# A linear-attention and token/channel mixer kernel: both first batches' units ahead of the first channel steps, group 0 split around group 1, w_ch1 loaded by step

## The chip, the cores and the metric

One Trainium2 chip; the program runs on one of its cores. The metric is device time in microseconds (us), the median of three runs. The inputs are single precision, the four weight matrices double precision.

## What is computed

```python
q_s = softmax(q, axis=-1)                          # q, k, v: (8, 8, 576, 64)
k_s = softmax(k, axis=2)
kv = np.einsum('bhsd,bhse->bhde', k_s, v)
x = np.einsum('bhsd,bhde->bhse', q_s, kv)          # then (8, 576, 512)
xt = x.transpose(0, 2, 1)
h = np.maximum(xt @ w_tok1, 0.0) @ w_tok2          # 576 -> 256 -> 576
u = x + h.transpose(0, 2, 1)
h2 = np.maximum(u @ w_ch1, 0.0) @ w_ch2            # 512 -> 1536 -> 512
return (u + h2).astype(np.float32)
```

The softmaxes are written out in the reference with a maximum, exponential and a sum plus 1e-9.

## The kernel before

**Units.** Attention and the token mixing are done per unit: a batch b and a pair j of heads, 128 columns of the 512. There are 8 x 4 = 32 units, numbered n = 4 b + j. A unit loads kt, q, k and v (`load_unit`), does the softmaxes (`softmax_k`, `softmax_q`, together `soft`), and then has four stages on TensorE (PE), `pe_stages`: s1 turns q and forms kv, s2 is the product with w_tok1, s3 the hidden layer and the first part of u, s4 the second part of u. Values are split into a high and a low part (`split`: an ACT copy, a VectorE subtraction), and each product is three matmuls. Units 0 to 7 (`on_pe`) transpose k and q on PE and do all subtractions on VectorE (DVE); the later ones turn q on DVE (L262, L270) and give two tensor operations, k_t (L202) and ql (L89), to GpSimd (POOL).

**Groups and steps.** The channel mixing runs over the 8 x 576 = 4608 tokens in nine groups of 512. A batch has 576 tokens, so group g needs u of batch g and, from group 1 on, of the batch before. A group has 12 channel steps f: `ch1` is 12 matmuls of 512 wide into a bank ps_h, then a ReLU on ACT (h2h) and DVE's low part (h2l, L344); `ch2` is 12 matmuls onto four banks ps_o, which hold the group's sums over all twelve steps. ch2 runs one step behind ch1. At the end `residual` adds u's two parts on POOL into a staging tile, and `out_end` adds the bank on DVE and writes out.

**Weights.** Each weight piece (128 x 512 doubles, 512 KB, 29 pieces) goes into a staging tile and is narrowed by five DVE passes and one of ACT (`narrow`, L143 to L150), then split (ACT and DVE). w_ch1 lies in c1h and c1l by rows of 512 columns, w_ch2 by step.

**Order.** Units 0 to 3 come first, with w_tok1, w_tok2 and the first quarter of w_ch1. Then group by group: the units of batch g + 1 are spread over the steps of group g by the table `todo` (one every three steps), and during group 0 each step also loads one piece of w_ch2 and, for eight steps, one of w_ch1. The program is written in that order; a scheduler sets the final order of each engine's queue, and every queue, SP's of loads among them, runs in order. v has a ring of two tiles. Staging and narrowing buffers: two, and two more in pools (`stg_more`, `cv_more`) that are closed when the space is needed. The names and lines that the prediction follows are the DVE passes above, h2l (L344), hl (L296), ul (L329), POOL's ql, k_t and residual (L360), and v_ring.

Of the kernel before, what the change touches and what calls it, by code (L numbers as in the profile page):

```python
# [12 lines left out]
ALU = mybir.AluOpType  # L13
# [7 lines left out]
def attn_mixer_kernel(ctx: ExitStack, tc: tile.TileContext, q, k, kt, v, wt, out, dims):  # L21
# [24 lines left out]
    upool = ctx.enter_context(tc.tile_pool(name="upool", bufs=3))  # L46
# [31 lines left out]
    c1h = const.tile([P, NJ, DCH], F32R, name="c1h")  # L78
    c1l = const.tile([P, NJ, DCH], F32R, name="c1l")
# [145 lines left out]
    def stage_kv(u):  # L225
        kx, vt = u["k"], u["v"]
# [72 lines left out]
    uT = {}  # L299

    def u_tiles(g):
        if g not in uT:
            uT[g] = tuple(upool.tile([P, NJ, CW], F32R, name="u" + part) for part in "hl")
        return uT[g]

    def stage_u(u, half):
# [40 lines left out]
    def ch2(acc, f, hh, hl):  # L347
# [197 lines left out]
```

## Time and profile before

| | |
|---|---|
| median of 3 runs | 860.49 us (858.84 to 860.98) |
| the profiled execution | 860.69 us, span 858.6 us |
| PE matmuls | busy 814.3 us (95%), 4224 instructions |
| DVE | busy 494.7 us (58%), 1093 |
| ACT | busy 335.6 us (39%), 785 |
| POOL | busy 124.4 us (14%), 98 |
| DMA | 63.5 MB, mean 74 GB/s |
| mean granted TensorE clock | 0.982 |

Shares are means over a program with two parts: in the first fifth DVE is full and PE is not, later it is the other way. Matmuls overlap, and a busy PE need not be at its peak; the distance between the starts of matmuls says more than their durations. The same holds for DVE, where an instruction's duration is some 0.07 us longer than the distance to the next start.

### The profile page before, as it was taken

How to read it: one execution, taken by the hardware profiler on the slowest of the kernel's cores; microseconds unless marked ns; L12 is line 12 of the kernel's file. 1: busy time of each engine (PE TensorE's matmuls, PEld its weight loads, DVE VectorE, ACT ScalarE, POOL GpSimd, SP SyncE). 2: the span in 40 equal slices, each digit the busy share in tenths (PEclk: the TensorE clock that was granted, in tenths of full speed). 3: DMA queues.
4: the chain of work that ended last, by engine and by line, in shares of the span. 5: the costliest groups of instructions: out<-in, count | busy, mean ns of one | idle time of the engine just before them, and what ended most of it. 6: DMA issues, size and time to landing. Idle time of an engine off the chain costs nothing.

```text
span 858.6 us, 11201 instructions
## 1 busy us (share of the span) xinstructions
PE 814.3 (95%) x4224; PEld 695.5 (81%) x4224; DVE 494.7 (58%) x1093; ACT 335.6 (39%) x785; POOL 124.4 (14%) x98
## 2 busy tenths in 40 slices
PE   3668999998999999999999999999999999999997
PEld 2567787877888888888888888888888888888886
DVE  7999998966555755485557555765556332112112
ACT  5676664534434444344444443444434331111100
POOL 0000000422011411041113111311132102001100
PEclk9689999999999999999999999999999999999999
DMA  8435444331112311131122112321121001001001
GB/s 285 133 100 179 146 129 162 94 109 60 60 60 71 99 47 55 37 108 61 60 59 98 59 60 60 110 61 60 45 94 45 1 1 50 1 0 50 1 1 49
DMA packets 41685, 63.50 MB, mean 74 GB/s; under 512 B 3488, under 2 KB 22048, under 8 KB 41632
## 3 DMA queue, kind: packets, MB, share of 16 engines
q1 hardware_dynamic: 36448, 53.36, 19.8%
q10 hardware_dynamic: 5184, 9.44, 2.9%
q8 instruction: 33, 0.54, 0.3%
q14 instruction: 20, 0.16, 0.1%
HBM read 53.35 MB, written 9.44 MB: 73 GB/s over the span
## 4 chain that ended last, share of the span: by engine, by line
PE 79%; DVE 13%; DMA 4%; issue 1%; ACT 1%; POOL 1%; SPq 0%; DVEq 0%; POOLq 0%; ACTq 0%
PE ps_h L341 31%; PE ps_o L352 31%; PE ps_h L322 7%; PE ps_h L281 5%; PE ps_h L229 3%; DMA stg<-in_w 2%; DVE cv_s L145 1%; PE ps_h L289 1%; DVE stg L148 1%; DVE cv_s L150 1%; DVE q_t L270 1%; DMA q_t<-in_q 1%; DVE stg L146 1%; DVE cv_s L143 1%; DVE q_t L212 1%
## 5 line engine op out<-in xcount | busy, mean ns | idle before, releaser
L344 DVE SCALAR_TENSOR_TENSOR h2l<-ps_h,h2h 128x512 fp32r<-128x512 f32 x108 | 74.2, 687 | 182.9 <-ACT h2h L343 182.9
L341 PE MATMUL ps_h<-uh,c1h 128*128 128x512 f32 x432 | 172.6, 400 | 0.9 <-ACT k_t L193 0.7
L341 PE MATMUL ps_h<-ul,c1h 128*128 128x512 f32 x432 | 171.7, 397 | 0.4 <-DVE ul L329 0.4
L341 PE MATMUL ps_h<-uh,c1l 128*128 128x512 f32 x432 | 171.4, 397 | 0.0
L352 PE MATMUL ps_o<-h2h,c2l 128*128 128x512 f32 x432 | 169.0, 391 | 0.0
L343 ACT ACTIVATE h2h<-ps_h 128x512 fp32r<-128x512 f32 x108 | 64.4, 597 | 261.1 <-PE ps_h L341 250.5
L352 PE MATMUL ps_o<-h2h,c2h 128*128 128x512 f32 x432 | 165.1, 393 | 1.5 <-DVE stg L367 1.5
L352 PE MATMUL ps_o<-h2l,c2h 128*128 128x512 f32 x432 | 157.3, 396 | 0.0
L270 DVE COPY q_t<-cv_s 32x160 f32<-32x160 f32 (+1 forms) x264 | 73.3, 278 | 69.9 <-POOL ql L89 66.7
L202 POOL TENSOR_TENSOR k_t<-k_t,mb 128x640 f32<-128x640 f32 x24 | 37.7, 1572 | 459.7 <-ACT mb L201 307.6
L341 PEld LDWEIGHTS ps_h<-ul,c1h 128*128 128x128 f32 x432 | 82.0, 190 | 19.8 <-DVE ul L329 0.6
L341 PEld LDWEIGHTS ps_h<-uh,c1h 128*128 128x128 f32 x432 | 82.2, 190 | 17.5 <-ACT k_t L193 0.9
L352 PEld LDWEIGHTS ps_o<-h2h,c2h 128*128 128x128 f32 x432 | 80.7, 188 | 18.6 <-DVE stg L367 2.6
L341 PEld LDWEIGHTS ps_h<-uh,c1l 128*128 128x128 f32 x432 | 82.2, 190 | 16.5
L352 PEld LDWEIGHTS ps_o<-h2h,c2l 128*128 128x128 f32 x432 | 81.1, 188 | 16.1
L352 PEld LDWEIGHTS ps_o<-h2l,c2h 128*128 128x128 f32 x432 | 79.5, 188 | 15.7
L360 POOL TENSOR_TENSOR stg<-uh,ul 128x512 f32<-128x512 f32 x36 | 47.5, 1343 | 128.4 <-DMA out<-stg 76.6
L211 DVE TENSOR_REDUCE st<-q_t 128x10 f32<-128x640 f32 x32 | 26.2, 819 | 43.8 <-DMA q_t<-in_q 43.8
L89 POOL TENSOR_TENSOR ql<-q_t,qh 128x640 fp32r<-128x640 f32 x24 | 37.9, 1581 | 83.7 <-ACT qh L88 64.1
L229 PEld LDWEIGHTS ps_h<-v_ring,k_t 128*128 128x128 f32 x320 | 44.5, 203 | 4.7 <-ACT qtl L253 2.0
L229 PE MATMUL ps_h<-v_ring,k_t 128*128 128x129 f32 x320 | 46.0, 289 | 1.4 <-ACT qtl L253 1.4
L213 ACT ACTIVATE q_t<-q_t 128x640 f32<-128x640 f32 x32 | 23.7, 740 | 49.7 <-DVE q_t L212 49.7
(136 smaller groups left out, 1223.3 us busy)
## 6 DMA issues: line engine op xcount, KB each, us to landing
stg<-in_w SPq DMA_DIRECT2D x28, 512.0 KB, 3.8
kt_t<-in_kt SPq DMA_DIRECT2D x32, 320.0 KB, 3.2
q_t<-in_q SPq DMA_DIRECT2D x32, 320.0 KB, 2.9
out<-stg ACTq DMA_DIRECT2D x36, 256.0 KB, 2.2
v_ring<-in_v SPq DMA_DIRECT2D x32, 256.0 KB, 2.9
k_t<-in_k SPq DMA_DIRECT2D x24, 320.0 KB, 3.4
v_ring<-in_v SPq DMA_DIRECT2D x32, 32.0 KB, 3.1
stg<-in_w SPq DMA_DIRECT2D x1, 256.0 KB, 6.2
```

Of the source, the lines that this page charges most:

```text
L89: lo_eng.tensor_tensor(lo, src, f32(hi), op=ALU.subtract)
L202: nc.gpsimd.tensor_tensor(kx, kx, mb.unsqueeze(1).broadcast_to([P, C1, P]), op=ALU.subtract)
L211: nc.vector.tensor_reduce(st[:, 0, :], qt, axis=AX.X, op=ALU.max)
L229: nc.tensor.matmul(kv[:, 0 : P + 1], kx[:, c, :], vt[:, c, 0 : P + 1], start=(c == 0), stop=(c == C))
L270: eng(qx[ys, 0:n, xs], turned[xs, 0:n, ys])
L281: nc.tensor.matmul(y[:, 0:TOK], a, w, start=(i == 0), stop=(i == len(mm) - 1))
L322: nc.tensor.matmul(t[:, 0:N], a, w, start=(i == 0), stop=(i == len(mm) - 1))
L341: nc.tensor.matmul(t, a[:, n, fs], w, start=(i == 0), stop=(i == 3 * NJ - 1))
L343: nc.scalar.activation(hh, t, AF.Relu)
L344: nc.vector.scalar_tensor_tensor(hl, t, 0.0, f32(hh), op0=ALU.max, op1=ALU.subtract)
L352: nc.tensor.matmul(o, a[:, cs], w, start=(f == 0 and i == 0), stop=(f == NF - 1 and i == 2))
L360: nc.gpsimd.tensor_tensor(res[n // 2][:, n % 2, :], f32(uh), f32(ul), op=ALU.add)
```

## The change

Units 0 to 7, both first batches, come before the first channel step. The steps are then a list: the first four of group 0 (`F_HEAD`), all twelve of group 1, the other eight of group 0, and groups 2 to 8 as before. Group 0's sums of its first four steps are copied by ACT from the banks to a tile `part`; POOL adds u's two parts to it, and the sums of the other eight are added at the end. The units of batch 2 begin ten steps before group 2 and come every two steps; later ones as before. A step's columns of w_ch1 form one piece, and `load_ch(f)` loads that and w_ch2's piece together: two such pairs among the units, one in each of the four first steps, and one in each of the first six of group 1. There is one v tile instead of two, loaded after the kv matmuls of the unit before; the first part has three staging buffers instead of four; the u tiles get fixed slots.

```diff
-    NE = NJ
-    N_PE = 2 * NJ
-    F_MORE = 8
+    NE = 2 * NJ
+    F_HEAD, F_MORE = 4, 8
...
-    NV = 2
-    v_ring = [const.tile([P, C1, P + 1], F32, name=f"v_ring{i}") for i in range(NV)]
+    v_t = const.tile([P, C1, P + 1], F32, name="v_t")
...
+    c2_rows(0, F_HEAD)
+    part = const.tile([P, NJ, CW], F32, name="part")
...
+    def load_v(n):
+        if n < NU:
+            nc.sync.dma_start(v_t[:, 0:C, 0:P], v[n][:, 0:C, :])
+            nc.sync.dma_start(v_t[0:TL, C, 0:P], v[n][0:TL, C, :])
...
+    def load_ch(f):
+        h_, l_ = (w[:, f].rearrange("p n m -> p (n m)") for w in (c1h, c1l))
+        split(h_, l_, load_weights(AT_C1 + f), nc.vector)
         split(*c2[f], load_weights(AT_C2 + f), nc.vector)
...
             nc.tensor.matmul(kv[:, 0 : P + 1], kx[:, c, :], vt[:, c, 0 : P + 1], start=(c == 0), stop=(c == C))
+        load_v(u["n"] + 1)
...
+        uh, ul = (x[:, n, :] for x in uT[g])
+        if g == 0:
+            t = part[:, n, :]
+            nc.gpsimd.tensor_tensor(t, t, f32(uh), op=ALU.add)
+            nc.gpsimd.tensor_tensor(t, t, f32(ul), op=ALU.add)
+            res[n] = t
+            return
...
-    def out_end(g, acc):
+    def out_end(g, acc, whole):
         for n, o in enumerate(acc):
-            t = res[n // 2][:, n % 2, :]
-            nc.vector.tensor_tensor(t, o, t, op=ALU.add)
-            nc.scalar.dma_start(out[g, n], t)
+            if not whole:
+                nc.scalar.copy(part[:, n, :], o)
+                continue
+            nc.vector.tensor_tensor(res[n], o, res[n], op=ALU.add)
+            nc.scalar.dma_start(out[g, n], res[n])
...
+    stg_more = early_pools.enter_context(tc.tile_pool(name="stg_more", bufs=1))
+    conv[:] = [(stg, cv), (stg, cv), (stg_more, cv)]
...
-        if n == NE - 2:
-            load_ch1(0, range(NJ))
+        if n >= NE - 3 and n < NE - 1:
+            load_ch(n - (NE - 3))
...
+    steps = [(0, f) for f in range(F_HEAD)] + [(1, f) for f in range(NF)] + [(0, f) for f in range(F_HEAD, NF)]
+    n0 = len(steps)
+    steps += [(g, f) for g in range(2, NG) for f in range(NF)]
...
+        if b == 2:
+            at = (n0 - 10, n0 - 9, n0 - 9, n0 - 8) if j == 0 else [n0 - 9.5 + 2 * j + x for x in (0, 0.5, 1, 1.5)]
+        else:
+            at = [n0 + (b - 3) * NF + 3 * j + x for x in (0, 1, 1.5, 2)]
...
+    for i, (g, f) in enumerate(steps):
+        if to_load < NF and (i < F_HEAD or g == 1):
...
+            load_ch(to_load)
+            to_load += 1
```

The order of the instructions shows the move. On PE, where the first channel step begins: before, this is behind unit 2 and in the middle of unit 3 (L281 and L322 are a unit's stages, L252 its transposes, L341 is ch1).

```order
L322 MATMUL ps_h<-w2h,hl 128x256
L289 MATMUL ps_h<-kvf,ys 128x128 x2
L322 MATMUL ps_o<-qth,kvh 128x320
L322 MATMUL ps_o<-qtl,kvh 128x320
L322 MATMUL ps_h<-qth,kvh 128x256
L322 MATMUL ps_h<-qtl,kvh 128x256
L341 MATMUL ps_h<-uh,c1h 128x512
L341 MATMUL ps_h<-uh,c1l 128x512
L341 MATMUL ps_h<-ul,c1h 128x512
```

In the change it is in the middle of unit 7, with one operation of unit 8 (L205) already ahead of it; L327 is the unit's stage, L345 is ch1.

```order
L327 MATMUL ps_h<-w2h,hl 128x256
L296 MATMUL ps_h<-kvf,ys 128x128 x2
L327 MATMUL ps_o<-qth,kvh 128x320
L327 MATMUL ps_o<-qtl,kvh 128x320
L327 MATMUL ps_h<-qth,kvh 128x256
L327 MATMUL ps_h<-qtl,kvh 128x256
L205 MATMUL ps_o<-dg,ones 128x128
L345 MATMUL ps_h<-uh_115,c1h 128x512
L345 MATMUL ps_h<-uh_115,c1l 128x512
L345 MATMUL ps_h<-ul_116,c1h 128x512
```

The same ten matmuls of a unit's end stand there, four units later.

On POOL, its first operations on tensors before: k_t and ql of units 8 and 9, and between them the residuals of group 0 (the first two pairs) and of group 1 (the third and fourth).

```order
L202 TENSOR_TENSOR k_t<-k_t,mb 128x640
L360 TENSOR_TENSOR stg<-uh,ul 128x512 x2
L89 TENSOR_TENSOR ql<-q_t,qh 128x640
L360 TENSOR_TENSOR stg<-uh,ul 128x512 x2
L202 TENSOR_TENSOR k_t<-k_t,mb 128x640
L360 TENSOR_TENSOR stg<-uh,ul 128x512 x2
L89 TENSOR_TENSOR ql<-q_t,qh 128x640
L360 TENSOR_TENSOR stg<-uh,ul 128x512 x2
```

In the change: ql and k_t of unit 8, eight additions onto part, four residuals of group 1, k_t and ql of unit 9, and one residual of group 2 at a time.

```order
L97 TENSOR_TENSOR ql<-q_t,qh 128x640
L208 TENSOR_TENSOR k_t<-k_t,mb 128x640
L363 TENSOR_TENSOR part<-part,uh_115 128x512 x3
L364 TENSOR_TENSOR part<-part,ul_116 128x512
L363 TENSOR_TENSOR part<-part,uh_115 128x512
L364 TENSOR_TENSOR part<-part,ul_116 128x512 x3
L370 TENSOR_TENSOR stg<-uh_117,ul_118 128x512 x4
L208 TENSOR_TENSOR k_t<-k_t,mb 128x640
L97 TENSOR_TENSOR ql<-q_t,qh 128x640
L370 TENSOR_TENSOR stg<-uh_119,ul_120 128x512
L208 TENSOR_TENSOR k_t<-k_t,mb 128x640
L97 TENSOR_TENSOR ql<-q_t,qh 128x640
```

Where pairs of residuals stood around unit 9's ql, four additions stand ahead of it, and four more instructions ahead of those.

On DVE, around the change's first h2l (L348; L334 is ul, of unit 7 here, the others are weight passes):

```order
L348 SCALAR_TENSOR_TENSOR h2l<-ps_h,h2h 128x512
L154 SCALAR_TENSOR_TENSOR cv_s<-stg,cv_s 128x512
L152 TENSOR_SCALAR cv_s<-stg 128x512
L334 TENSOR_TENSOR ul_118<-ps_o,uh_117 128x320
L157 SCALAR_TENSOR_TENSOR stg<-stg 128x512
L154 SCALAR_TENSOR_TENSOR cv_s<-stg,cv_s 128x512
L334 TENSOR_TENSOR ul_118<-ps_h,uh_117 128x128
```

This h2l is instruction 232 of DVE's queue counted with repeats; before, the first h2l is instruction 174, and from the first to the thirteenth h2l the change has 119 instructions.

## Rows read from the trace of the kernel before

**Rows 1.** The page: the span in 40 slices of 21.5 us, busy tenths and granted clock

```profile
PE   3668999998999999999999999999999999999997
...
DVE  7999998966555755485557555765556332112112
...
PEclk9689999999999999999999999999999999999999
```

**Rows 2.** Stretches: us, busy us (count) of PE, PEld, DVE, ACT, POOL, clock, DMA, GB/s

```profile
20.00:40.00 20.00, 13.66 (x61) 11.86 (x62) 20.00 (x47) 13.52 (x28) 0.00 (x0) 0.57 0.41 133
740.00:760.00 20.00, 20.00 (x88) 16.22 (x88) 2.20 (x4) 2.39 (x4) 0.00 (x0) 1.00 0.00 1
```

**Rows 3.** Who PE waited for, 0 to 200 us: us in total, times, longest

```profile
PE ps_h L289 <- ACT kvf L236: 7.7, 2, 5.7
...
PE ps_o L352 <- DVE stg L367: 1.5, 3, 0.6
```

**Rows 4.** Timeline of PE, last matmul of units 7 to 10: start us, us, what

```profile
170.97 0.28 PE L322 MATMUL ps_h<-w2h,hl 128*128 128x256 f32 x1
...
199.37 0.30 PE L322 MATMUL ps_h<-w2h,hl 128*128 128x256 f32 x1
...
223.38 0.28 PE L322 MATMUL ps_h<-w2h,hl 128*128 128x256 f32 x1
...
245.85 0.28 PE L322 MATMUL ps_h<-w2h,hl 128*128 128x256 f32 x1
```

**Rows 5.** Timeline of POOL, DVE and PE behind group 0 [idle before it, and until whom]

```profile
188.93 2.54 POOL L360 TENSOR_TENSOR stg<-uh,ul 128x512 f32<-128x512 f32 x2 [6.90 <-DMA out<-stg]
...
193.01 4.80 DVE L270 COPY q_t<-cv_s 32x160 f32<-32x160 f32 x11 [4.72 <-POOL ql L89]
...
198.33 0.41 PE L322 MATMUL ps_h<-w2h,hl 128*128 128x320 f32 x1 [2.17 <-DVE hl L296]
```

**Rows 6.** Timeline of DVE around the first step's h2l

```profile
82.55 0.68 DVE L344 SCALAR_TENSOR_TENSOR h2l<-ps_h,h2h 128x512 fp32r<-128x512 f32 x1
83.16 0.42 DVE L143 TENSOR_SCALAR cv_s<-stg 128x512 uint32<-128x512 uint32 x1
...
84.16 0.80 DVE L182 TENSOR_REDUCE mc<-kt_t 128x1 f32<-128x640 f32 x1
84.88 0.68 DVE L150 TENSOR_TENSOR cv_s<-stg,cv_s 128x512 f32<-128x512 f32 x1
```

**Rows 7.** Stretch up to 170.97 us, ch1 (L341) alone, then ch2 (L352) alone

```profile
0.00:170.97 170.97, 37.72 (x144) 27.39 (x144) 0.92 0.48 154
...
0.00:170.97 170.97, 32.86 (x127) 22.78 (x127) 0.92 0.48 154
```

**Rows 8.** Timeline of POOL and of DVE, 160 to 169 us

```profile
160.50 2.72 POOL L360 TENSOR_TENSOR stg<-uh,ul 128x512 f32<-128x512 f32 x2 [4.40 <-DVE cv_s L150]
163.18 2.01 POOL L89 TENSOR_TENSOR ql<-q_t,qh 128x640 fp32r<-128x640 f32 x1
166.42 3.00 POOL L360 TENSOR_TENSOR stg<-uh,ul 128x512 f32<-128x512 f32 x2 [1.23 <-DVE cv_s L150]
...
160.93 1.14 DVE L146 TENSOR_SCALAR stg<-stg 128x512 uint32<-128x512 uint32 x1
162.11 1.67 DVE L148 SCALAR_TENSOR_TENSOR stg<-stg 128x512 f32<-128x512 uint32 x1
163.70 2.04 DVE L89 TENSOR_TENSOR c2l<-cv_s,c2h 128x512 fp32r<-128x512 f32 x1
...
167.03 1.24 DVE L89 TENSOR_TENSOR c2l<-cv_s,c2h 128x512 fp32r<-128x512 f32 x1
```

**Rows 9.** Tile v_ring, its DMAs; kv matmuls of units 2 and 3 on PE

```profile
DMA to landing us min/median/max: 2.6/3.0/7.3
...
48.31 1.28 PE L229 MATMUL ps_h<-v_ring,k_t 128*128 128x129 f32 x10
...
61.18 2.15 PE L229 MATMUL ps_h<-v_ring,k_t 128*128 128x129 f32 x10
```

More of the change, by code (lines that the diff above doesn't have):

```diff
@@ L297, in stage_h1 @@
         u["hh"], u["hl"] = hh, hl
[L299 to L304, printed above, removed]
+    slots = [tuple(upool.tile([P, NJ, CW], F32R, name=f"u{x}{i}") for x in "hl") for i in range(3)]
+    uT = [slots[i] for i in (0, 1, 2, 1, 0, 2, 1, 0, 2)]
+    assert len(uT) == NG
     def stage_u(u, half):
@@ L345, in ch1, with ch2 @@
         return hh, hl
-    def ch2(acc, f, hh, hl):
+    def ch2(acc, f, first, last, hh, hl):
         for n, o in enumerate(acc):
@@ L414, in attn_mixer_kernel @@
     begin(1)
[L415 removed]
     for n in range(NE):
[L417 removed]
+        st = pe_stages(n)
         st[0]()
         begin(n + 2)
[L420 removed]
+        if n + 1 < NE:
+            soft(n + 1)
         st[1]()
@@ new lines, in attn_mixer_kernel @@
+    for n in range(NE, NU):
+        b, j = divmod(n, NJ)
+        if b == 2:
+            at = (n0 - 10, n0 - 9, n0 - 9, n0 - 8) if j == 0 else [n0 - 9.5 + 2 * j + x for x in (0, 0.5, 1, 1.5)]
+        else:
+            at = [n0 + (b - 3) * NF + 3 * j + x for x in (0, 1, 1.5, 2)]
+        s1, s2, s3, s4 = pe_stages(n)
+        put(at[0], s1)
+        put(at[0], lambda n=n: soft(n + 1))
+        put(at[0] + 0.5, lambda n=n: begin(n + 2))
+        for x, fn in zip(at[1:], (s2, s3, s4)):
+            put(x, fn)
@@ new lines, in attn_mixer_kernel @@
+    pend = None
+    to_load = 2
+    for i, (g, f) in enumerate(steps):
+        if to_load < NF and (i < F_HEAD or g == 1):
+            if to_load == F_MORE:
+                more_pools.close()
+                conv[:] = [(stg, cv)]
+                c2_rows(F_MORE, NF)
+            load_ch(to_load)
+            to_load += 1
+        h = ch1(g, f)
+        for fn in todo.pop(i, []):
+            fn()
+        if pend is not None:
+            ch2(*pend[1:])
+            if pend[0] != g:
+                out_end(*pend[:2], i != F_HEAD)
+        for fn in todo.pop(i + 0.5, []):
+            fn()
+        last = i + 1 == len(steps) or steps[i + 1][0] != g
+        if pend is None or pend[0] != g:
+            acc = [ps_o.tile([P, CW], F32, name="ps_o") for _ in range(NJ)]
+        pend = (g, acc, f, pend is None or pend[0] != g, last, *h)
+        if last and i != F_HEAD - 1:
+            for n in range(NJ):
+                residual(g, n)
@@ L502, in pieces @@
     cut += list(tail)
-    for x in range(0, w_ch1.shape[1], CW):
-        cut += list(w_ch1[:, x : x + CW].reshape(-1, P, CW))
+    n, f = (x // P for x in w_ch1.shape)
+    cut += list(w_ch1.reshape(n, P, f, P).transpose(2, 1, 0, 3).reshape(f, P, CW))
     cut += list(w_ch2.reshape(-1, P, CW))
```

116 lines of the change are left out of this document (31 added, 85 removed).

## The prediction

> **What bounds the kernel now.** I read the page's first two parts, then stretches of 20 us, then who PE waited for, then single lines around the places that these pointed to.
>
> The slices show two stretches: for the first eight DVE is at 9 of 10 or nearly, and PE is short of it in the first four; behind the ninth PE stands at 9 to the end and DVE eases [rows 1]. From 20 to 40 us DVE is busy for all 20 us, PE for 13.66 at a granted clock of 0.57; from 740 to 760 us PE is busy throughout at 1.00, with 88 matmuls, one start every 0.227 us [rows 2]. What fills DVE is narrowing the double-precision weights (six passes a piece and one to split it) and the softmaxes of the first units. So there is a front of some 170 us paced by DVE, and then a long stretch paced by PE. The change has exactly as many matmuls of each shape, so only the front and the hand-over can give time.
>
> PE's waits of the first 200 us are many and small, the largest 7.7 us on kvf [rows 3]. They are links of one chain behind DVE's order; removing one alone gives nothing.
>
> The hand-over shows in the last matmul of each unit: 170.97 us for unit 7, 199.37, 223.38 and 245.85 for units 8 to 10 [rows 4]. The last step is 22.5 us, that of the steady part (three channel steps and a unit); the two before it are 28.4 and 24.0. So 5.9 + 1.5 = **7.4 us are lost around the end of group 0**. How can be read: POOL starts on the residual of group 1 at 188.93, after 6.90 us for an output's DMA to free the staging buffer; the ql of the next unit stands behind it; DVE waits 4.72 us for that ql, then copies the turned q for 4.80 us; hl comes behind the copies, and PE, which had idled 2.17 us for hl, goes on at 198.33 [rows 5].
>
> **The change, step by step.** The profiled execution took 860.69 us with a span of 858.6; the median of the three runs, 860.49, is 0.2 below it, so I sum against 860.7 and take the result for the median's.
>
> *Units 4 to 7 before the first step.* DVE reaches the first step's h2l at 82.55 us [rows 6]. In its order this is the 174th instruction, in the change the 232nd. The 58 more are 21 of 640 wide (6 maxima of kt, 6 reductions and 6 products on q, 3 ql), 5 weight passes (3 long, 2 short), 4 hl, 9 ul, 4 kvl and 15 of a few elements. Start to start, a 640-wide one takes 0.72 us, a 512-wide one 0.61, a short pass some 0.35 (0.42, of which 0.07 overlap) [rows 6]: 15.1 + 1.8 + 0.7, and for the narrow ones, scaled by width, an estimated 1.3 + 2.4 + 0.8 + 2.0. That is 24.1 us; 58 at the full window's mean (47 in 20 us [rows 2]) give 24.7. DVE has no idle time there to absorb it, so the first h2l moves by 24.3 to **106.9 us**. Unit 7's last matmul feeds, by an ACT copy, a ul that stands six rows, some 3 us, behind this h2l: it runs at about 109 us.
>
> *The steps after it.* When unit 7's last matmul runs today, at 170.97 us, PE has issued all 8 units and 144 + 127 = 271 of the steps' matmuls [rows 7]. In the change it has the 8 units and 12 of those at 109 us and needs 259 more: at 0.227 us, 58.8. If nothing stops it, it stands at 167.8 us where it now stands at 170.97: 3.1 us won. Over the same twelve steps DVE has, by its order, some 74 long passes, 28 short ones, and one unit's turning and splitting of about 6 us: 45 + 10 + 6 = 61 us. The two are level: PE no longer starves for weights, and has no slack either.
>
> *POOL beside DVE.* Eight additions onto group 0's kept sums stand where four residuals were, and come in the middle of the weight splitting, with one ql and one k_t. Between 160.5 and 169.4 us POOL ran five instructions beside weight passes, and four of DVE's took 1.14, 1.67, 2.04 and 1.24 us [rows 8] where such passes alone take 0.42 and 0.68 [rows 6]: 0.72 + 0.99 + 1.36 + 0.56 = 3.6 us more, 0.73 for each of POOL's. Ten are 7.3 us, so DVE has 68 us beside PE's 59. A good part hides, since DVE's passes for a step are due a step or more later; I take 2.5 us, the bounds are 0 and 9.
>
> The Trainium skill, SBUF — State Buffer, section Who interferes with whom, speaks against this part: VectorE and GpSimd share one port pair as an exclusive lock, and whichever comes second is blocked fully, not slowed. By it each addition would cost DVE its whole length, and the time would be the fourth rival's; the trace agrees for single passes (2.04 us is 1.36 more than alone) and not for the mean (0.73).
>
> *One v tile instead of two.* The load of the next unit's v now waits for this unit's kv matmuls. It lands in 3.0 us, 7.3 at worst; kv matmuls in the front are 12.9 us apart [rows 9], and units 4 to 7 add some 24.3 us of DVE for four, with weights between, so about 8 apart. It fits unless SP's queue, which is in order, stands on another wait when the load is due. Bounds: 0, and seven loads by 3.0 us, 21. I take 1.5, as 8 leaves more than one landing over.
>
> *Three staging buffers in the front instead of four; w_ch1 by step.* Number and size of the pieces stay, and DVE idled for none from 20 to 40 us [rows 2]. Nothing; what a late piece costs is in the rival on loads.
>
> *Keeping group 0's sums.* Four ACT copies of 128x512 after the fourth step. ACT is busy for 13.5 of 20 us where it is fullest [rows 2], and PE needs those banks again only after two more ch1. Nothing.
>
> *The hand-over.* POOL's queue still holds the residual of group 1 ahead of a unit's k_t and ql, but directly behind the last weights, when no output is under way, and that of group 2 comes one addition at a time between units. The wait on an output's DMA has no counterpart, and the 7.4 us go. Two irregular ends of groups remain (group 1 to the rest of group 0, and that to group 2), where DVE's additions can hold PE as today (1.5 us in three waits [rows 3]): 1 us for both, bounds 0 and 3.
>
> **Sum.** 860.7 - 3.1 + 2.5 + 1.5 - 7.4 + 1.0 = 855.2, say **855.0 us**. With all three added terms at nothing it is 850; 860 with contention at 6 and the others at 2.
>
> **Rivals.**
> 1. *As above*, 855.0 us (851 to 860): chance 0.57.
> 2. *All covers hold*: no contention, no late load, nothing lost at either end: 850.2, and some less if the added units fill the few us that DVE idled before 82 us; 848 to 851. For it: PE and DVE are level in the steps. Against: DVE would have to go 100 us without a wait. Chance 0.13.
> 3. *Loads come late*: SP's queue holds v behind weight pieces whose buffers DVE frees late. For it: one v tile and three buffers leave fewer loads ahead. Against: DVE was full from 20 to 40 us with the same queue. Three late loads of 3.0 us each [rows 9] add 9: 864. Chance 0.12.
> 4. *POOL blocks DVE fully*: ten instructions by 1.27 us at least (two in 2.54 [rows 5]) are 13 us; DVE has 74 us beside 59, the twelfth step comes 15 us behind instead of 2.5: 867, less what can wait, about 865. Against: the mean of the five was half of it [rows 8]. Chance 0.09.
> 5. *Slower by the clock*: in the front PE has short bursts, and the granted clock was 0.57 from 20 to 40 us [rows 2] and 0.8 to 0.9 in the two slices after [rows 1]. The front now lasts 24 us longer. Eight units are about 52 us of PE at full clock (a steady period of 22.5 us less 72 matmuls of a step by 0.227 is 6.1, and some 0.4 for the transposes that the first eight make on PE); with the first step's ch1 55, of which I put 10 before 40 us. From 40 to 109 us 45 remain, so a clock under 0.65 makes PE, not DVE, the pace. At 0.57 they take 79 us instead of 69: 865, slower than today, and 0.05 less adds 8. Against: a mix of units and weights had 0.8 and more from 43 us on. Chance 0.09. The Trainium skill, TensorE: Matmul & The Clock Gate, Part 1, says that the throttled clock is the default and activity releases it; by it the time would be this rival's, and the trace agrees in that a sparse stretch had the low level for part of it (0.57).
>
> That the change doesn't do what it says is no rival: the order of the instructions shows it.
>
> **Chances and range.** 0.3% (2.6 us) is about what a measurement of this kernel can tell from no change. Faster, under 857.9: most of the first case (0.43), the second (0.13), a little of the third (0.02): 0.58. The same: the rest of the first (0.14), half of the third (0.06), a third of the fourth (0.03): 0.23. Slower: 0.19. The range from 848 to 866 takes in cases 1 and 2, most of 3 and 4, and leaves out lower clocks and the bad end of the loads.
>
> **What would show it.** Right: the first h2l at 105 to 109 us; PE full from there; no step of 28 us between units 8 to 11 that a wait on POOL explains; DVE passes of 1 us and more beside the additions onto part. Wrong: DVE idle for a DMA between 20 and 110 us; a granted clock under 0.65 from 40 to 105 us; PE idle for 2 us or more at a time after 110 us; a first h2l after 112 us.

## The result and the profile after

The changed kernel took **861.47 us** (median of 16 runs, 858.56 to 864.1), the kernel before 859.9 us (16 runs, 857.9 to 860.98). The ratio is 1.0025 with a 95% interval of 1.0015 to 1.0034: 0.25% slower, where 855.0 us, 0.6% faster, had been forecast. The spans of the two profiled executions differ by 0.5 us (859.1 after, 858.6 before).

The slices of the page, first (busy tenths in 40 slices of 21.5 us, and the granted clock):

```profile
PE   3587898999999999999999999999999999999997
...
DVE  7999899895776555475557555665556332112112
...
POOL 0000107032221111131113111311122102001100
PEclk9988999999999999999999999999999999999999
```

Where PE before reached 9 in the fifth slice and stayed there but for one 8 [rows 1], it now reaches it in the sixth, drops to 8 in the seventh (129 to 150 us), and stays at 9 from the eighth. In the seventh POOL is busy for 7 tenths. In stretches of 20 us (columns as in [rows 2]):

```profile
20.00:40.00 20.00, 12.41 (x64) 10.52 (x62) 19.70 (x47) 12.77 (x28) 0.00 (x0) 1.00 0.40 124
120.00:140.00 20.00, 20.00 (x88) 16.22 (x87) 20.00 (x36) 11.69 (x19) 7.16 (x3) 1.00 0.44 158
140.00:160.00 20.00, 17.56 (x71) 13.96 (x70) 18.91 (x24) 5.91 (x10) 9.10 (x6) 0.91 0.16 53
180.00:200.00 20.00, 19.36 (x96) 16.00 (x97) 15.25 (x32) 7.26 (x17) 5.06 (x3) 1.00 0.23 65
```

From 120 to 140 us PE does what the steady part does, 88 matmuls in 20 us [rows 2]. In the next 20 us it does 71, and DVE, though busy for 18.91 us, gets through 24 instructions instead of 36, while POOL is at work for 9.10.

To follow where time goes I count PE's **lost time**: the length of a stretch less its matmuls, each at the distance from start to start that its shape has at full clock (0.231 us for 512 columns, 0.148 for 320, 0.12 for 256, 0.109 for 129, 0.072 for 128, worked out from the starts in the traces). In us, from the one profiled execution of each kernel (the middle rows are the experiments below):

| kernel | 0-140 | 140-180 | 180-220 | 220-840 |
|---|---|---|---|---|
| before | 55.5 | 1.2 | 6.6 | 5.0 |
| **the change** | 55.6 | **4.9** | 1.2 | **7.3** |
| additions late, in staging (e1) | 56.7 | 0.0 | 3.8 | 7.5 |
| whole groups (e2) | 55.8 | 1.0 | 1.9 | 5.4 |
| twice the additions (e3) | 55.6 | 11.8 | 2.1 | 8.4 |
| before, one ql on DVE (e4) | 54.7 | 1.5 | 4.5 | 5.0 |
| residuals in part (e5) | 57.2 | 4.0 | 1.8 | 4.6 |
| sums behind the weights (e8) | 56.3 | 0.0 | 4.2 | 4.7 |
| whole groups, own tile (e9) | 56.0 | 1.2 | 1.9 | 4.5 |
| unit 8 held back (e10) | 49.5 | 4.7 | 2.1 | 8.4 |
| e9 with unit 8 held back (e12) | 51.5 | 0.8 | 2.0 | 4.5 |
| additions on DVE (e13) | 54.6 | 0.0 | 0.6 | 6.6 |
| e13, e5 and e10 together (e14) | 49.7 | 0.1 | 4.0 | 4.4 |

The eight kernels whose first 130 us are those of the change (it, e1, e2, e3, e5, e8, e9 and e13) differ by up to 2.6 us in the first column: so much does one execution vary. The other columns repeat better. The profiled execution was its kernel's fastest in e2, e8, e13 and e14 (2.6, 2.2, 1.2 and 2.3 us under the median), so their rows are a little better than their medians. Against before, the change lost 3.7 us more at 140 to 180, won 5.4 at 180 to 220, and lost 2.3 more behind that: the first two were terms of the sum, the third was not.

**At 137 to 150 us.** The timeline of POOL (start us, us, what, count):

```profile
132.84 8.31 POOL L363 TENSOR_TENSOR part<-part,uh 128x512 f32<-128x512 f32 x3 [25.20 <-ACT part L377]
141.11 1.75 POOL L364 TENSOR_TENSOR part<-part,ul 128x512 f32<-128x512 f32 x1
142.82 1.74 POOL L363 TENSOR_TENSOR part<-part,uh 128x512 f32<-128x512 f32 x1
144.52 4.58 POOL L364 TENSOR_TENSOR part<-part,ul 128x512 f32<-128x512 f32 x3
```

and of DVE in the same time:

```profile
136.77 0.68 DVE L348 SCALAR_TENSOR_TENSOR h2l<-ps_h,h2h 128x512 fp32r<-128x512 f32 x1
137.37 0.93 DVE L152 TENSOR_SCALAR cv_s<-stg 128x512 uint32<-128x512 uint32 x1
138.22 1.79 DVE L154 SCALAR_TENSOR_TENSOR cv_s<-stg,cv_s 128x512 uint32<-128x512 uint32 x1
139.93 1.78 DVE L159 TENSOR_TENSOR cv_s<-stg,cv_s 128x512 f32<-128x512 f32 x1
141.63 1.78 DVE L97 TENSOR_TENSOR c1l<-cv_s,c1h 128x512 fp32r<-128x512 f32 x1
143.33 1.51 DVE L155 TENSOR_SCALAR stg<-stg 128x512 uint32<-128x512 uint32 x1
144.76 1.78 DVE L154 SCALAR_TENSOR_TENSOR cv_s<-stg,cv_s 128x512 uint32<-128x512 uint32 x1
146.47 1.51 DVE L152 TENSOR_SCALAR cv_s<-stg 128x512 uint32<-128x512 uint32 x1
147.90 1.75 DVE L157 SCALAR_TENSOR_TENSOR stg<-stg 128x512 f32<-128x512 uint32 x1
149.57 0.68 DVE L348 SCALAR_TENSOR_TENSOR h2l<-ps_h,h2h 128x512 fp32r<-128x512 f32 x1
```

The eight passes between the two h2l took 12.2 us (137.37 to 149.57). Alone they take 0.34 or 0.60 us from start to start, 4.0 us in all. So eight additions cost DVE **8.2 us, 1.0 us each**, in one piece. PE, from its timeline, waited for the h2l at the end and then ran slow for a while:

```profile
147.48 0.39 PE L356 MATMUL ps_o<-h2h,c2l 128*128 128x512 f32 x1
150.31 1.65 PE L356 MATMUL ps_o<-h2l,c2h 128*128 128x512 f32 x3 [2.44 <-DVE h2l L348]
151.75 0.63 PE L356 MATMUL ps_o<-h2h,c2h 128*128 128x512 f32 x1
152.18 0.63 PE L356 MATMUL ps_o<-h2h,c2l 128*128 128x512 f32 x1
```

Behind the gap matmuls start 0.43 us apart instead of 0.23 (the granted clock of the stretch is 0.91), so the 2.6 us of the gap became 4.1 us lost from 140 to 160.

**Ahead of the first step.** The timelines of POOL and DVE show the same twice, and the first h2l at 111.76 us:

```profile
91.02 1.56 POOL L97 TENSOR_TENSOR ql<-q_t,qh 128x640 fp32r<-128x640 f32 x1 [88.87 <-DMA kt_t<-in_kt]
106.08 1.56 POOL L208 TENSOR_TENSOR k_t<-k_t,mb 128x640 f32<-128x640 f32 x1 [13.51 <-ACT mb L207]
...
91.18 1.68 DVE L152 TENSOR_SCALAR cv_s<-stg 128x512 uint32<-128x512 uint32 x1
106.43 1.50 DVE L152 TENSOR_SCALAR cv_s<-stg 128x512 uint32<-128x512 uint32 x1 [0.38 <-DMA stg<-in_w]
111.76 0.68 DVE L348 SCALAR_TENSOR_TENSOR h2l<-ps_h,h2h 128x512 fp32r<-128x512 f32 x1
```

The ql and k_t of unit 8 stretch two passes from 0.42 us [rows 6] to 1.68 and 1.50.

**The hand-over.** The last matmuls of units 7 to 10 (as [rows 4]):

```profile
110.05 0.27 PE L327 MATMUL ps_h<-w2h,hl 128*128 128x256 f32 x1
210.56 0.28 PE L327 MATMUL ps_h<-w2h,hl 128*128 128x256 f32 x1
227.51 0.28 PE L327 MATMUL ps_h<-w2h,hl 128*128 128x256 f32 x1
244.45 0.28 PE L327 MATMUL ps_h<-w2h,hl 128*128 128x256 f32 x1
```

The units of batch 2 now come 17.0 us apart, which is two channel steps (48 matmuls by 0.231 us) and the 5.8 us of a unit (22.4 us of the steady period less 72 matmuls): nothing is lost between them.

**The late part.** Two ends of groups, at 379 and 560 us, have a stall that the kernel before has not. The second, from the timelines of POOL, DVE and PE:

```profile
550.54 2.54 POOL L370 TENSOR_TENSOR stg<-uh,ul 128x512 f32<-128x512 f32 x2 [5.44 <-DMA out<-stg]
...
554.63 4.80 DVE L277 COPY q_t<-cv_s 32x160 f32<-32x160 f32 x11 [4.57 <-POOL ql L97]
...
559.94 0.39 PE L327 MATMUL ps_h<-w2h,hl 128*128 128x256 f32 x1 [1.29 <-DVE hl L303]
```

It is the chain of [rows 5]: a residual that waits for an output's DMA, a ql behind it, DVE's copies behind that, hl behind the copies.

### The profile page after: what moved, and what is told of

Its sections match the earlier page's. It is cut to its first block, busy times and chain, and to the rows that moved or that the text cites. A ratio compares the mean times of both kernels' runs of the same rounds, so it can differ in the third digit from the quotient of the medians.

```text
span 859.1 us, 11232 instructions
## 1 busy us (share of the span) xinstructions
PE 813.2 (95%) x4224; PEld 695.8 (81%) x4224; DVE 498.8 (58%) x1093; ACT 337.2 (39%) x789; POOL 135.1 (16%) x100
## 4 chain that ended last, share of the span: by engine, by line
PE 79%; DVE 12%; DMA 4%; ACT 2%; issue 1%; POOL 1%; SPq 0%; DVEq 0%; ACTq 0%; POOLq 0%
PE ps_h L345 31%; PE ps_o L356 30%; PE ps_h L327 6%; PE ps_h L288 4%; PE ps_h L235 3%; PE ps_h L296 2%; DMA stg<-in_w 1%; DVE q_t L277 1%; DVE cv_s L154 1%; DVE stg L157 1%; DVE cv_s L159 1%; DMA out<-stg 1%; DVE cv_s L152 1%; PE ps_o L288 1%; DVE stg L155 1%
## 5 line engine op out<-in xcount | busy, mean ns | idle before, releaser
L348 DVE SCALAR_TENSOR_TENSOR h2l<-ps_h,h2h 128x512 fp32r<-128x512 f32 x108 | 74.1, 687 | 182.4 <-ACT h2h L347 182.4
L345 PE MATMUL ps_h<-uh,c1h 128*128 128x512 f32 x432 | 171.2, 396 | 0.0
L345 PE MATMUL ps_h<-ul,c1h 128*128 128x512 f32 x432 | 170.4, 395 | 0.0
L345 PE MATMUL ps_h<-uh,c1l 128*128 128x512 f32 x432 | 170.4, 394 | 0.0
L356 PE MATMUL ps_o<-h2h,c2h 128*128 128x512 f32 x432 | 169.5, 393 | 0.0
L356 PE MATMUL ps_o<-h2l,c2h 128*128 128x512 f32 x432 | 154.2, 399 | 3.7 <-DVE h2l L348 3.7
L277 DVE COPY q_t<-cv_s 32x160 f32<-32x160 f32 (+1 forms) x264 | 68.4, 259 | 68.2 <-POOL ql L97 64.9
L345 PEld LDWEIGHTS ps_h<-ul,c1h 128*128 128x128 f32 x432 | 81.3, 188 | 19.1
L345 PEld LDWEIGHTS ps_h<-uh,c1l 128*128 128x128 f32 x432 | 81.6, 189 | 16.9
L345 PEld LDWEIGHTS ps_h<-uh,c1h 128*128 128x128 f32 x432 | 81.5, 189 | 16.6
L370 POOL TENSOR_TENSOR stg<-uh,ul 128x512 f32<-128x512 f32 x32 | 41.9, 1332 | 180.3 <-DMA out<-stg 76.1
L235 PEld LDWEIGHTS ps_h<-v_t,k_t 128*128 128x128 f32 x320 | 42.2, 196 | 3.0 <-DVE ul L334 0.8
L235 PE MATMUL ps_h<-v_t,k_t 128*128 128x129 f32 x320 | 43.5, 280 | 0.7 <-DVE ul L334 0.7
L219 ACT ACTIVATE q_t<-q_t 128x640 f32<-128x640 f32 x32 | 23.7, 741 | 49.5 <-DVE q_t L218 49.5
```

What stands on the lines that cost most here:

```text
L277: eng(qx[ys, 0:n, xs], turned[xs, 0:n, ys])
L345: nc.tensor.matmul(t, a[:, f, n, :], w, start=(i == 0), stop=(i == 3 * NJ - 1))
L348: nc.vector.scalar_tensor_tensor(hl, t, 0.0, f32(hh), op0=ALU.max, op1=ALU.subtract)
L356: nc.tensor.matmul(o, a[:, cs], w, start=(first and i == 0), stop=(last and i == 2))
L370: nc.gpsimd.tensor_tensor(res[n], f32(uh), f32(ul), op=ALU.add)
```

## The experiments

Each is timed in five rounds against the kernel before, and ratios are to the runs of before on the same chip. The theory, **A**: a POOL instruction beside weight passes stops DVE for about 1 us, in the middle and in the front. Its rivals: weights that come late, the split order as such, the eight units in the front as such, and new waits that take the place of what is removed.

### e1: the additions behind the last weights

```diff
...
         if n % 2 == 0:
             t = stg.tile([P, CW, 2], U32, name="stg")...
             res[n], res[n + 1] = t[:, 0:CW], t[:, CW : 2 * CW]
+        if g == 0:
+            nc.gpsimd.tensor_tensor(res[n], part[:, n, :], f32(uh), op=ALU.add)
+            nc.gpsimd.tensor_tensor(res[n], res[n], f32(ul), op=ALU.add)
+            return
```

The lines that add onto `part` in place go.

> The changed kernel (861.5 us) with one edit: group 0's eight additions write into two staging tiles instead of in place, so they can only run when the last weight piece has left its tile. Theory A (the additions stop DVE): between 137.4 and 149.6 us eight weight passes took 12.2 us where they take 4.0 start to start without the additions; PE lost 4.1 us from 140 to 160 us. Those 8.2 us of DVE go, every pass from 130 to 160 us is back at 0.7 us or less, PE is busy for over 19.5 us from 140 to 160, and the time is 857 to 858. Theory B (weights late): the late h2l at 149.6 us came from the staging buffers, for which DVE waited 3.4 us between 158 and 169 us; then those waits stay or move forward, and the time stays within 1 us of 861.5. Theory C (a new wait): the additions, now behind the output of group 1, hold POOL's queue ahead of a unit's k_t and ql, and 2 to 5 us are lost after 180 us: 860 to 863.

Measured: 861.02 us, ratio 1.0009 (0.9996 to 1.0023), not A's 857 to 858. At 140 to 180 us PE lost nothing (4.9 before the edit): theory A holds there, and B falls, for the weights' staging buffers are as they were. But at 200 to 240 us 5.6 us were lost, as C had it. The stretch of this run:

```profile
200.00:220.00 20.00, 17.11 (x96) 14.54 (x95) 15.90 (x24) 8.44 (x21) 14.25 (x10) 0.99 0.37 118
```

and POOL's, DVE's and PE's timelines in it:

```profile
203.98 2.54 POOL L365 TENSOR_TENSOR stg<-part,uh 128x512 f32<-128x512 f32 x2 [6.43 <-DMA out<-stg]
...
213.29 2.13 POOL L208 TENSOR_TENSOR k_t<-k_t,mb 128x640 f32<-128x640 f32 x1
...
217.00 2.11 DVE L223 TENSOR_TENSOR q_t<-q_t,st 128x640 f32<-128x640 f32 x1
...
219.77 1.65 PE L356 MATMUL ps_o<-h2l,c2h 128*128 128x512 f32 x3 [2.31 <-DVE h2l L348]
```

The additions wait 6.43 us for an output's DMA, POOL is then busy for 14.25 of 20 us, and the next unit's k_t comes behind seven of the eight. A softmax on DVE runs beside all this and is stretched (L223 took 2.11 us, alone 0.82), and PE waits 2.31 us for the h2l behind it. One stop was removed and another made.

### e2: whole groups

```diff
-    steps = [(0, f) for f in range(F_HEAD)] + [(1, f) for f in range(NF)] + [(0, f) for f in range(F_HEAD, NF)]
+    steps = [(g, f) for g in range(2) for f in range(NF)]
-        if to_load < NF and (i < F_HEAD or g == 1):
+        if to_load < NF:
-        if last and i != F_HEAD - 1:
+        if last:
```

The copies to `part` and the additions onto it go too.

> The changed kernel with the order of the steps undone: group 0 is run whole, then group 1; no sums are kept and no additions onto them are made; units 4 to 7 still stand before the first step, w_ch1 still comes by step. Theory A (additions stop DVE): the 4.1 us lost from 140 to 160 us go, as in the run with late additions, and no end of a group is irregular: 856 to 858. If group 1's residual again waits for group 0's output with a ql behind it, as in the kernel before (5.9 us on one unit), part of that comes back: 858 to 861. Theory D (it is the eight units in the front that cost, not the split order): no more than 1 us is won, 860.5 to 861.5, and the first h2l stays at 111 to 112 us in every case.

Measured: 858.96 us, ratio 0.9984 (0.9971 to 0.9997); the first h2l at 112.4 us, 1.0 us lost from 140 to 180. That is 0.4% under the change, theory A's second line. What stays of the change, the eight units in the front and w_ch1 by step, is a small gain on the kernel before (0.16%), not a loss: D falls. From 180 to 220 us it loses 1.9 us, against 6.6 before: most of what the change won at the hand-over doesn't need the split order.

### e3: twice the additions

```diff
             nc.gpsimd.tensor_tensor(t, t, f32(ul), op=ALU.add)
+            nc.gpsimd.tensor_tensor(t, t, f32(ul), op=ALU.subtract)
+            nc.gpsimd.tensor_tensor(t, t, f32(ul), op=ALU.add)
```

> The changed kernel with sixteen POOL instructions where eight add onto the kept sums (a subtraction and an addition more for each part, of the same tile). Theory A (each POOL instruction beside weight passes stops DVE for about 1 us): DVE's stretched passes last 8 us longer, about sixteen of 1.5 to 1.8 us; DVE has no slack left behind the first eight, so PE loses 6 to 8 us more and the time is 867 to 870. Theory B (weights late, POOL harmless): within 1 us of 861.5. In between, by the mean of 0.73 us that the prediction took for each: 5.8 us on DVE, 865 to 867.

Measured: 870.29 us, ratio 1.0116 (1.0099 to 1.0134), by the ratios 7.8 us above the change, and at the upper edge of A. The stretch:

```profile
140.00:160.00 20.00, 14.49 (x57) 11.43 (x56) 20.00 (x16) 3.67 (x6) 20.00 (x13) 0.91 0.14 53
```

and three rows of DVE's timeline in it:

```profile
151.04 1.75 DVE L157 SCALAR_TENSOR_TENSOR stg<-stg 128x512 f32<-128x512 uint32 x1
152.71 0.68 DVE L348 SCALAR_TENSOR_TENSOR h2l<-ps_h,h2h 128x512 fp32r<-128x512 f32 x1
153.31 0.89 DVE L155 TENSOR_SCALAR stg<-stg 128x512 uint32<-128x512 uint32 x1
```

From 134.85 to 160.65 us DVE made sixteen passes and two h2l. Less the two h2l (1.2 us) that is 24.6 us for passes that take 8.3 alone (eleven by 0.60, five by 0.34): 16.3 us for sixteen additions, again 1.0 us each.

### e4: the kernel before with one ql on DVE

```diff
-        split(qh, ql, qc, nc.vector if u["on_pe"] else nc.gpsimd)
+        split(qh, ql, qc, nc.vector if u["n"] in (*range(N_PE), N_PE + 1) else nc.gpsimd)
```

> The kernel before (859.9 us) with one instruction moved: the ql of the second unit of group 1's steps is made by DVE (640 wide, some 0.7 us) instead of POOL, where it stood behind a residual that waited 6.9 us for an output's DMA. Theory E (that wait is what the hand-over lost): DVE's idle 4.72 us before its copies goes, the step of 28.4 us of that unit becomes 23 to 24, and the time 855 to 856.5. Theory F (another wait takes its place: the k_t of the next unit still stands behind the same residuals, and its h2l and hl behind DVE's copies): the step stays over 26 us, and the time is over 858.

Measured: 856.9 us, ratio 0.9959 (0.9944 to 0.9974). The waiting goes, as E says, but the copies now run beside the residuals themselves (DVE's and POOL's timelines):

```profile
189.13 0.83 DVE L89 TENSOR_TENSOR ql<-q_t,qh 128x640 fp32r<-128x640 f32 x1 [0.63 <-ACT qh L88]
189.99 6.66 DVE L270 COPY q_t<-cv_s 32x160 f32<-32x160 f32 x11
...
189.31 5.54 POOL L360 TENSOR_TENSOR stg<-uh,ul 128x512 f32<-128x512 f32 x4 [7.08 <-DMA out<-stg]
```

Eleven copies took 6.66 us beside four residuals; in e1, with POOL idle, eleven took 2.73. So the unit's step fell from 28.4 to 27.9 us only (F, as to the step), the next from 24.0 to 22.5. The time lies between E's 855 to 856.5 and F's 858. One moved instruction does more for the kernel before than the change does.

### e5: later residuals in the tile of the kept sums

```diff
-        if n % 2 == 0:
+        if g % 2 == 0:
+            res[n] = part[:, n, :]
+        elif n % 2 == 0:
```

> The changed kernel with one edit: the residuals of groups 2, 4, 6 and 8 are written into the tile of the kept sums, which is free by then, instead of a staging tile that an output's DMA must leave first. Additions onto the kept sums stay where they are. Theory G (the wait on an output's DMA at every other end of a group costs in the late part, and by its length varies from run to run): PE's stalls of 0.9 us at 378.9 and 1.6 us at 559.9 us, each behind a ql that stood behind such a residual, become fewer, 1 to 2.5 us are won (859 to 860.5), and the times of the runs lie closer together than 858.6 to 864.1. Rival: these stalls are hidden or random; within 0.5 us of 861.5.

Measured: 858.63 us, ratio 0.9991 (0.9982 to 1.0000), runs from 857.95 to 859.93. From 340 us on PE waits for nothing that the profile shows, and behind 220 us it lost 4.6 us instead of 7.3. G holds, by a little more than expected: 0.34% of 859.5, **2.9 us** (by the two intervals 1.8 to 4.0), is what the outputs' DMAs cost the change behind the hand-over, and with them most of the spread goes.

### e8: the sums added behind the weights, ahead of group 1's residual

```diff
+            s = sums[n // 2][:, n % 2 * CW : (n % 2 + 1) * CW]
+            nc.gpsimd.tensor_tensor(s, f32(uh), f32(ul), op=ALU.add)
+            nc.gpsimd.tensor_tensor(part[:, n, :], part[:, n, :], s, op=ALU.add)
...
+        if i == 10:
+            sums = [stg.tile([P, CW, 2], U32, name="stg")... for _ in range(2)]
+            for n in range(NJ):
+                residual(0, n)
```

It also has e5's edit.

> The changed kernel with group 0's part u added to the kept sums behind the last weights, as in the run with late additions, but through two staging tiles that are free again at once, and ahead of group 1's residual, so that no output's DMA stands before them; residuals of the later even groups go into the tile of the kept sums. Theory A with C (additions beside weight passes cost 4 to 5 us of PE; the run with late additions gave them back at 200 to 240 us, 5.6 us, because they waited 6.4 us for an output's DMA with a k_t behind them): both losses go, PE loses under 1 us from 140 to 180 and under 3 us from 180 to 240, and the time is 855 to 857.5. Rival H (the additions cost as much wherever they stand, since DVE copies and softmaxes of the next units are stopped instead): 859 to 861.5.

Measured: 859.75 us, ratio 1.0002 (0.9991 to 1.0013), the H case. Nothing was lost from 140 to 180 us, 4.2 us from 180 to 220. POOL's and DVE's timelines:

```profile
174.10 3.03 POOL L363 TENSOR_TENSOR stg<-uh,ul 128x512 f32<-128x512 f32 x2
177.10 2.54 POOL L364 TENSOR_TENSOR part<-part,stg 128x512 f32<-128x512 f32 x2
...
174.76 6.42 DVE L277 COPY q_t<-cv_s 32x160 f32<-32x160 f32 x10
```

Now it is the copies of the turned q that are stopped, 6.42 us for ten. Against e5, whose edit it has, the move won nothing (1.0002 and 0.9991). In each of the three places tried, here, in e1 and in the change, the additions on POOL stopped DVE work that a step waited for.

### e9: whole groups with a tile of their own for later residuals

```diff
+    own = const.tile([P, NJ, CW], F32, name="own")
-        if n % 2 == 0:
+        if g > 0 and g % 2 == 0:
+            res[n] = own[:, n, :]
+        elif n % 2 == 0:
```

> The kernel with whole groups (859.0 us, units 4 to 7 first) with a tile of its own for the residuals of groups 2, 4, 6 and 8. Theory G (outputs' DMAs hold the residuals, and with them ql, in the late part): 1 to 2 us less, 857 to 858, and a smaller spread than 856.3 to 861.3. Rival: no change, 859. Against the run with sums behind the weights: if that is no faster than this one, keeping sums and splitting group 0 has no gain of its own.

Measured: 855.4 us (853.73 to 856.24), ratio 0.9954 (0.9942 to 0.9966), 0.3% better than e2 and 0.5% better than e8. The time is below G's 857 to 858; the traces show only 0.9 us won behind 220 us (the table), and e2's, of its fastest execution, has stalls of only 0.5 us there. So G points the right way, but that it explains all of the gain isn't shown. With the additions on POOL, the split order has no gain of its own.

### e10: unit 8 held back

```diff
+        late = f32(c2[10][1][:, 0:1]) if n == NE else None
...
+        if late is not None:
+            nc.scalar.copy(t[:, 0:1], late)
...
-    soft(NE)
+    put(8, lambda: begin(NE))
+    put(9, lambda: begin(NE + 1))
+    put(11, lambda: soft(NE))
```

> The changed kernel with the loads and softmax of the ninth unit held back until one of the last weight pieces is split (three copies of 128x1 on ACT write into its tiles first; its input is then loaded over them), so that its k_t and ql on POOL and some nine instructions on DVE leave the front. Theory A (POOL instructions stop DVE; two of 1.56 us stretched two passes to 1.68 and 1.50 us from 0.42): 2.3 us of DVE for the stops and 3 to 4 us for the nine instructions go, the first h2l comes at 105 to 107 us instead of 111.8, and since DVE sets the front the time falls by most of it, 855 to 858; the stop at 137 to 150 us stays and moves with the rest. Theory B (front set by waits on loads: DVE idled 2.7 us more than before): first h2l not before 109 us, time 859 to 861.5. Theory I (the held-back unit comes late for its own step): a stall of 3 us or more on its transposes or kv behind the last weights, 860 to 864.

Measured: 857.07 us, ratio 0.9974 (0.9965 to 0.9984). The first h2l, from DVE's timeline:

```profile
105.66 0.68 DVE L355 SCALAR_TENSOR_TENSOR h2l<-ps_h,h2h 128x512 fp32r<-128x512 f32 x1
```

It is 6.1 us earlier, in A's range, and PE lost 49.5 us by 140 us instead of 55.6. The stop by the additions stays (4.7 us). B falls, and so does the stall that I had named, though 0.9 us more was lost from 180 to 220 us and 1.1 behind that.

### e13: the additions on DVE

```diff
-            nc.gpsimd.tensor_tensor(t, t, f32(uh), op=ALU.add)
-            nc.gpsimd.tensor_tensor(t, t, f32(ul), op=ALU.add)
+            nc.vector.tensor_tensor(t, t, f32(uh), op=ALU.add)
+            nc.vector.tensor_tensor(t, t, f32(ul), op=ALU.add)
```

> The changed kernel with the eight additions onto the kept sums made by DVE itself instead of POOL. Theory A (beside weight passes a POOL instruction stops DVE for about its own length: eight passes took 12.2 us instead of 4.0): DVE then pays eight times some 0.61 us, 4.9 us, instead of 8.2 us; no pass takes over 1 us between 125 and 150 us, PE loses 1 to 2 us from 140 to 160 instead of 4.1, and the time is 858 to 860. If POOL only shared DVE's time (0.73 us for each, as the prediction took), the two would cost about the same, 5.8 against 4.9 us, and the time stays between 860.5 and 861.5.

Measured: **855.13 us**, ratio 0.9961 (0.9948 to 0.9975). DVE's timeline:

```profile
133.58 2.49 DVE L363 TENSOR_TENSOR part<-part,uh 128x512 f32<-128x512 f32 x4
...
138.73 2.49 DVE L364 TENSOR_TENSOR part<-part,ul 128x512 f32<-128x512 f32 x4
```

and the stretch:

```profile
140.00:160.00 20.00, 20.00 (x88) 16.30 (x87) 16.88 (x32) 7.45 (x12) 0.00 (x0) 1.00 0.21 71
```

This tells most. DVE does the work itself in 4.8 us, no pass near it is stretched, and PE loses nothing at all from 140 to 180 us; I had expected 1 to 2, and 858 to 860 us. So DVE had some 5 us of slack there. From the last matmul of unit 7 PE runs 259 matmuls of steps in 59.88 us, 0.231 us each, without a stop:

```profile
109.18 0.27 PE L327 MATMUL ps_h<-w2h,hl 128*128 128x256 f32 x1
...
169.06 0.62 PE L356 MATMUL ps_o<-h2l,c2h 128*128 128x512 f32 x2
```

Against the change the ratio falls by 0.0064, **5.5 us** (by the two intervals 4.1 to 6.9): that is the price of having the eight additions on POOL instead of DVE in this place.

### e12 and e14: the winning parts together

e12 is e9 with e10's edit, e14 the change with the edits of e5, e10 and e13.

> Whole groups, units 4 to 7 first, a tile of its own for the residuals of even groups (855.4 us), and the ninth unit held back as in the run that did that to the changed kernel (861.5 to 857.1 us). Theory A (two POOL instructions and nine of DVE's leave a front that DVE sets): the first h2l comes at 105 to 106 us and the two gains add up, 850 to 852. Theory I (with no additions to stop DVE, the front's gain meets the held-back unit's own step or the last weights, where 1.3 us are lost twice already): half of it is given back, 852.5 to 855.

> The changed kernel with the three edits that won alone put together: the eight additions on DVE (861.5 to 855.1 us), residuals of the later even groups in the tile of the kept sums (to 858.6), the ninth unit held back (to 857.1). Theory A (three separate losses: 6 us at 140 to 200, some 2.5 in the late part, 4 to 5 in the front): they add up, less what the front's lead gives back where DVE has the additions sooner, 847 to 850; and the split order with kept sums is then 2 to 4 us better than whole groups with the same two other edits (851.3). Theory I (DVE's slack behind the first step is used up by 4.9 us of additions and 4 of the held-back unit): PE loses 2 us or more between 110 and 200 us again, and the time is 850.5 to 853, no better than whole groups.

Measured: e12 **851.26 us** (849.7 to 851.98), ratio 0.9907 (0.9894 to 0.9921), the fastest of all and 0.9% under the kernel before; e14 853.03 us, ratio 0.9940 (0.9922 to 0.9958). In e12 the gains add up, though its first h2l came at 108.0 us instead of 105 to 106. In e14 they don't, and the time is at the upper edge of I's: nothing is lost up to 180 us, but 4.0 us from 180 to 220, where e13 alone lost 0.6. Between 110 and 240 us DVE waits 7.3 us in all for loads of q, and PE 2.6 us for unit 8's hh and hl: the held-back unit, as in I, but at its hidden layer and not where I had looked. The trace is of its fastest execution, 2.3 us under the median; what held the others isn't shown. Beside these edits the split order with kept sums brings nothing that whole groups don't. Without them, and with the additions on DVE, it does: e13 is 0.23% faster than e2 (0.9961 and 0.9984, with intervals that overlap by 0.0004), which also holds later residuals in staging tiles. Whether e13 with e5's edit alone would beat e9 wasn't run.

## Why the prediction was wrong

The forecast was 855.0 us; 861.47 was measured. Against before, the sum had -5.5 us and the medians say +1.6. By its steps:

- **"POOL beside DVE ... I take 2.5 us, the bounds are 0 and 9": this step failed, by 3 us.** The eight additions cost 5.5 us (e13 against the change; in the traces 4.9 from 140 to 180 us). Three things were wrong in it. The price of one was 1.0 us on DVE (e3 and the change), not 0.73: the mean over [rows 8] took in POOL instructions that stood beside fewer weight passes than these eight, and left out copies behind them that were stopped too (eleven took 3.48 us, as the line below shows, where they take 2.73 with POOL idle). "The two are level", with "no slack either", set DVE's 61 us for twelve steps beside 59 us of PE; but those are the 259 matmuls up to another moment, and twelve steps have 288, 66.4 us from the first h2l to the thirteenth in e13. So DVE had some 5 us of slack by the sum's own count, and 4.8 us of DVE additions hid wholly in e13. And "a good part hides" weighed sums over twelve steps, whereas the scheduler put all eight additions in a row, so that DVE fell 8.2 us behind within one step: that is more than the slack, and the slow clock behind PE's gap made 4.1 us of 2.6. The rule of the Trainium skill that I set against this step (SBUF — State Buffer, Who interferes with whom: an exclusive lock, the second comer blocked fully) was nearer than my mean: 1.0 us of an addition's 1.28. The fourth rival's time, 865, was too high all the same, since it gave DVE too little slack. The copies, from DVE's timeline of the kernel before:

```profile
168.53 3.48 DVE L270 COPY q_t<-cv_s 32x160 f32<-32x160 f32 x11
```

- **"DVE has no idle time there to absorb it, so the first h2l moves by 24.3 to 106.9 us": failed, but it cost little.** It moved by 29.2, to 111.76 (110.7 to 113.2 in the eight kernels with this front). Missing were 2.3 us for the two passes beside unit 8's ql and k_t, which I had counted among the POOL instructions of the middle, and 2.7 us of idle time: the gaps between DVE's instructions up to the first h2l add up to 7.65 us, before 4.97, and the largest waits that before has not are 1.5 us in all for PE's kv and 1.2 for ACT's pass of the weights. The 24.2 us that are left agree with the 24.1 of the 58 instructions. But unit 7's last matmul, which I had put 2 us behind this h2l, at 109, came ahead of it, at 110.05, and from 110 to 140 us PE lost 0.1 us. What sets the time is the front as a whole: in e10 this h2l comes 6.1 us earlier and unit 7's last matmul 6.4, and 4.4 us were won.
- **"3.1 us won" by the steps:** not reached. PE had 271 of the steps' matmuls out at 173.95 us, against 167.8 forecast without the added terms: 1.0 us is the late start, 4.0 the additions' stop, and 1.1 a misreading of [rows 2]. The 88 matmuls there include those that only reach into the window at its edges; their starts are 0.231 us apart and not 0.227, so 259 take 59.9 us and not 58.8, and at most 2.1 us could be won. e13, with no stop, needs 59.88.
- **"The 7.4 us go" and "1 us for both" irregular ends: right in kind, a little high.** From 180 to 220 us the loss fell from 6.6 to 1.2 us, 5.4 won for 6.4. By e2 most of this comes with whole groups too.
- **Behind the hand-over nothing was in the sum: failed.** The change loses 2.3 us more there than the kernel before, at the ends of later groups; e5 takes the loss away (2.9 us in the medians' ratio). I had read the chain of a residual, an output's DMA and a ql once, at group 0, and called it gone; it is at later ends too, and at two of them PE waits for it. Why the split kernels hit it harder (6.6 to 8.4 us lost behind 220 us in the change, e1, e3, e10 and e13, which hold these residuals in staging tiles) than before and e2 (5.0 and 5.4) isn't settled; no run separates it.
- **One v tile, 1.5 us:** nothing. In the list of PE's waits up to 112 us no load of v appears. The staging buffers, at nothing, were right: DVE waits 3.4 us for pieces from 158 to 169 us, but e13, with the same buffers, loses nothing there. The copies of the kept sums on ACT, at nothing, too. So the spare 1.5 us hid part of the other misses, by luck.
- **The rivals.** Loads late (864) and the clock (865) are out: from 20 to 112 us DVE waited 1.3 us in all for loads, as before up to 90; PE had 0.83 and more from 40 us on, and DVE set the pace. POOL stopping DVE had the mechanism but was given 0.09.

By the traces, then, the change stood at 173.95 us where the sum, with its added terms, has 171.8: the late start (1.0), the spacing (1.1) and the additions (1.5 over their 2.5), less the 1.5 of the v tile. Behind that it lost some 4 us more than forecast: 1.0 at the hand-over, 2.3 in the late part, and 0.8 on an h2l at 179 us. The two traces differ by 0.5 us and the medians by 1.6; the last microsecond is that of the executions that were profiled.

Of the signs that I had named, a first h2l at 105 to 109 us was missed, PE was full only up to 147 us, and it idled for 2.44 us at 150; DVE passes of over 1 us beside the additions, and no unit step of 28 us, came as forecast.

## What to carry to other kernels

An instruction moved to a helper engine is not free because that engine is idle: look at what DVE does at that moment, and price it at most of its own length (here 1.0 us of DVE for an addition of 1.28); eight additions cost 5.5 us more on POOL than on DVE, the busier engine, where PE lost nothing by them. Where a scheduler places work that is only ready early, count where it really goes: a row of eight is not eight spread over twelve steps. A wait that is removed at one end of a loop should be looked for at every other end.

## What the runs showed that I had not expected

- Which DVE instructions are stopped. In e3, with POOL busy for 20.00 of 20 us, passes with two inputs in SBUF took 1.75 to 1.78 us and the one-input passes (L152, L155) 0.89 to 1.52, but h2l, with one input in a bank, took 0.68 as always. The Trainium skill, SBUF — State Buffer, Who interferes with whom, has this rule: a DVE instruction with two SBUF inputs contends with a GpSimd one that reads SBUF, one in a faster two-port mode contends too, and one with a single SBUF input outside these modes does not. The runs agree.
- The stops take turns. In the stopped stretch DVE's passes and POOL's additions both start 1.4 to 1.7 us apart, one of each in turn. But ahead of it POOL's first addition, which started at 132.84 us, took 5.17 us instead of 1.28, while DVE made seven passes from 133.09 on at their usual length. By its end it got in at about 136.7, where an h2l stood on DVE; so it did in e10, but in e3 it got in behind a short pass. What ends such a wait is not known.
- The copies of 32 partitions are stopped as well: eleven took 2.73 us with POOL idle, 6.66 beside four residuals.
